# One order for every engine from a plan instead of a table of slots, in a kernel of attention and two feed-forward blocks

## The chip, the cores and the metric

One Trainium2 core runs the whole program; nothing is exchanged with other cores. The time is the device time of one execution in microseconds (us). TensorE does the matrix products, VectorE and ScalarE the elementwise work and the reductions along a row, GpSimd small operations and a reduction over partitions; SyncE and GpSimd issue most of the DMA transfers. Each engine takes its instructions strictly in the order in which the program was written for it, and waits at the first that is not ready.

## The reference

```python
def _attn_ref(q, k, v):                      # 4 batches, 8 heads, 576 rows, 64 columns, f32
    q_rot, k_rot = (rotate(q), rotate(k))    # rotary embedding over the two halves of a row
    scores = scale * np.matmul(q_rot, k_rot.transpose(0, 1, 3, 2))
    scores = scores - np.max(scores, axis=-1, keepdims=True)
    attn = np.exp(scores)
    attn = attn / (np.sum(attn, axis=-1, keepdims=True) + 1e-09)
    return np.matmul(attn, v)

def _moe_ref(x, mu_k, mu_r, w_k, w_v, w_r):  # x is 4 x 576 x 512, w_k 512 x 1024, w_v 1024 x 512
    xk = mu_k * x + (1.0 - mu_k) * x_prev    # x_prev: x moved down by one row
    xr = mu_r * x + (1.0 - mu_r) * x_prev
    k = np.maximum(xk @ w_k, 0.0)
    v = k * k @ w_v
    return 1.0 / (1.0 + np.exp(-(xr @ w_r))) * v

def _moe2_ref(x, w_in, w_spatial, b_spatial, w_out):
    h = np.maximum(x @ w_in, 0.0)
    u, v = (h[..., :512], h[..., 512:])
    v_n = (v - mu) / np.sqrt(var + 1e-06)    # mean and variance of a row
    v_s = np.einsum('ts,bsd->btd', w_spatial, v_n) + b_spatial[None, :, None]
    return u * v_s @ w_out
```

## The kernel before

The program has two phases. The first, which the change is about, does attention and the products with w_k and w_v; the second does the rest and is written out further down in both kernels alike.

**Attention** goes by units. There are 72: 18 for each batch, and one holds 128 rows of a pair of heads (units 8 and 9 of a batch take the last 64 rows of two pairs each). Unit m takes these steps. `scores` (L244, TensorE) writes two PSUM tiles `s`; `top` (L250, VectorE) takes the largest value of each row, once for each head; `expo` (L255, ScalarE) the exponential; `norm` (L260, L261) the reciprocal of the row's sum; `high` (L267, ScalarE) and `low` (L271, VectorE) write the probabilities as two f16 parts into `p`; `turn` (L276) has SyncE issue a DMA transpose of `p` into `pt`; `values` (L296, TensorE, 36 or 72 matmuls, tile `pv`) multiplies by v; and after some units `gather` (L306 to L318) copies the sums to `xt` and stores them to `xd`. The scores of a unit need both `s` tiles of an earlier unit back, so they wait for its `expo`.

**Each pair of heads** is got ready before its units: `load` brings q and k (tiles `raw_0` and `raw_1`, 576 KB each, issued by GpSimd at L166, for the first pair by SyncE), `rope` (L171, L172, VectorE) rotates them into `rot`; at most two `raw` tiles of a kind of buffer are in use, so a load waits for an earlier `rope`. `v_load` (L176, SyncE) brings v into `vr`; `v_max` (L180, VectorE), a sum over partitions on GpSimd (L181), `v_scale` (L185, L186) and `v_split` (L193 on ScalarE, L194 on VectorE) write it as two f16 parts into `vv`, which SyncE copies to the other half of the partitions (L199, L200).

**The first feed-forward block**, `moe1(b, h)`, runs for one part h of a batch's rows (256 or 320) beside the attention of the next batch: `mix` (L340 to L347) writes `x`; `k_dot` (L355) does the product with w_k in eight groups of twelve matmuls (tile `mk`); `k_square` (L364 to L373) squares and splits into `kk`; `v_dot` (L385, tile `mv`) does the product with w_v; `v_out` copies the result to `vs`, and SyncE stores it (L393, `vd`). `vs` and the first tile of `mix` share three buffers. The 16 pieces of w_k and w_v are loaded as 64-bit words and put together at the start (L101 to L118; their last step, a subtraction, is GpSimd's).

**The order** comes from one list, `agenda`. Each step is added with a slot, a number on one scale for the whole phase, where unit m stands at m: its scores at m - .5, its `low` at m + 1.1, its transpose at m + 1.12, its values at m + 3.05. The list is sorted by slot, and every engine gets its steps in that order. The numbers were written by hand and say nothing about how long a step takes. The extra PSUM tiles `ps_x` serve the first units and give way to the pool `ps_m` of the feed-forward block.

Of the kernel before, what the change touches and what calls it, by code (L numbers as in the profile page):

```python
# [27 lines left out]
NX = 20  # L28
# [3 lines left out]
LAG = 3  # L32
# [4 lines left out]
def raw(ap):  # L37
    return ap.bitcast(F32)


@with_exitstack
def body(ctx: ExitStack, tc, qp, kp, vp, cs, mu_k, mu_r, w_k, w_v, w_r, w_in, w_sp, b_sp, w_out, out):
# [12 lines left out]
    st0p = ExitStack()  # L55
# [3 lines left out]
    ps_pv = att.enter_context(tc.tile_pool(name="ps_pv", bufs=1, space=PSUM, side="right"))  # L59

    moe = ph1.enter_context(tc.tile_pool(name="moe", bufs=1))
# [9 lines left out]
    def load_mix():  # L71
        nc.sync.dma_start(mix4[:, :, 0], mu_k.rearrange("(c p) -> p c", p=128))
        nc.sync.dma_start(mix4[:, :, 2], mu_r.rearrange("(c p) -> p c", p=128))
        for k in (0, 2):
            nc.vector.tensor_scalar(mix4[:, :, k + 1], mix4[:, :, k], -1.0, 1.0, op0=ALU.mult, op1=ALU.add)
    epsc = const.tile([128, 2], F32, name="epsc")
# [63 lines left out]


    agenda = []

    def add(slot, fn):
        agenda.append((slot, len(agenda), fn))

    def steps(gen, slots):
        for s in slots:
            add(s, lambda: next(gen, None))
# [5 lines left out]
    def prep(i, s):  # L155
# [22 lines left out]
        def v_max():  # L178
            vm = t["vm"] = at.tile([128, 4], F32, tag="vm", bufs=2, name=f"vm{i}")
            nc.vector.tensor_reduce(vm[:, 0:1], t["vr"], axis=AX.XY, op=ALU.max, apply_absolute_value=True)  # L180
            nc.gpsimd.partition_all_reduce(vm[:, 1:2], vm[:, 0:1], channels=128, reduce_op=bass_isa.ReduceOp.max)  # L181

        def v_scale():
            vm = t["vm"]
            nc.vector.tensor_scalar(vm[:, 2:3], vm[:, 1:2], 1e-30, 1.0 / P_SCALE, op0=ALU.max, op1=ALU.mult)  # L185
            nc.vector.reciprocal(vm[:, 3:4], vm[:, 2:3])  # L186
            nc.gpsimd.tensor_scalar(musc[:, b, p, :], mix4[:, p, :], vm[:, 2:3], 1.0 / P_SCALE, op0=ALU.mult, op1=ALU.mult)

        def v_split():
# [3 lines left out]
            nc.scalar.mul(v5[:, :, 0:D], vr, vm[:, 3:4])  # L193
            nc.vector.scalar_tensor_tensor(v5[:, :, D:], vr, vm[:, 3:4], v5[:, :, 0:D],  # L194
# [12 lines left out]
        todo = []  # L207
        for w in range(2):
            r = at_rope(2 * p + w)
            todo += [(r - 2, load, 1 - w, 0), (r - 1.99, load, 1 - w, 1), (r, rope, 1 - w)]  # L210
        todo += [(s - 3.5, v_load), (s - 2.57, v_max), (s - .57, v_scale), (s - .56, v_split), (s - .55, v_copy)]
        if i == 0:

            todo = [(-9, load, 1, 0), (-8.9, load, 1, 1), (-8.8, load, 0, 0), (-8.7, load, 0, 1), (-8.6, v_load),
                    (-8.5, rope, 1), (-8.4, rope, 0), (-8.3, v_max), (-2.6, load_mix), (.43, v_scale), (.44, v_split),
                    (.45, v_copy)]
        for d, fn, *arg in todo:
            add(d, lambda fn=fn, arg=arg: fn(*arg))
# [14 lines left out]
    def scores(m):  # L233
        ps = [(ps_x if n < NX and n % 3 == 2 else ps_s).tile([128, 2, 512], F32, tag="s", name=f"s{n}")
# [47 lines left out]
    def values(m):  # L282
        b, w = divmod(m, UN)
        pt = units.pop(m)
        if w in (0, 4, 8, 10, 14):
            pvt[0] = (ps_x if m == 4 else ps_pv).tile([128, 512], F32, tag="pv", name=f"pv{m}")
# [12 lines left out]
    def gather(m):  # L299
# [3 lines left out]
        for p in range(NP) if w == 9 else (0, 1) if w in (3, 13) else (2, 3):  # L303
# [5 lines left out]
            if w < 9:  # L309
                for h, (_, n) in enumerate(PART):  # L310
                    xt[i, h] = xpool.tile([128, 1 + n], F32, tag=f"xt{h}", bufs=NP, name=f"xt{i}_{h}")
                nc.gpsimd.memset(xt[i, 0][:, 0:1], 0.0)
                nc.scalar.copy(xt[i, 0][:, 1:], src)
                nc.gpsimd.tensor_copy(xt[i, 1][:, 0:1], xt[i, 0][:, 256:])
                nc.gpsimd.dma_start(x_dram[b][:, p, :257], xt[i, 0])
            else:
                nc.scalar.copy(xt[i, 1][:, 65:], src)
                nc.gpsimd.dma_start(x_dram[b][:, p, 257:], xt[i, 1][:, 1:])  # L318
# [7 lines left out]

    def ps_m():
        if "ps_m" not in pool:
            st0p.close()
            pool["ps_m"] = ph1p.enter_context(tc.tile_pool(name="ps_m", bufs=3, space=PSUM))  # L330
        return pool["ps_m"]
# [17 lines left out]
    def k_dot(b, h, fc):  # L349
        xh, xl = mo[b, h, "x"]  # L350
        ps = mo[b, h, "k", fc] = ps_m().tile([128, 512], F32, tag="m", name=f"mk{b}_{h}_{fc}")
        m = 0
        for c in range(NP):
# [23 lines left out]
    def v_dot(b, h, dc, half):  # L377
        if half == 0:
            mo[b, h, "v", dc] = ps_m().tile([128, 512], F32, tag="m", name=f"mv{b}_{h}_{dc}")
        ps = mo[b, h, "v", dc]  # L380
        m = 12 * half
        for fc in range(4 * half, 4 * half + 4):
# [5 lines left out]
    def v_out(b, h, dc):  # L388
# [4 lines left out]
        nc.sync.dma_start(v_dram[b][:, dc, o:o + n], vs)  # L393

    def moe1(b, h):

        end = UN * b + LAG + (17 if h else 7)
        s, places = end + 1.6, 16 if h else 20
        at_ = lambda m: s + .5 * int(m * places / 16)
        for c in range(NP):  # L400
            m = (end - 3.5 if c < 2 else end) + (c % 2)
            steps(mix(b, h, c), (end + .2, end + .41, end + .95, end + 1.08) if c == 2 else
                  (end + .42, end + .55, end + 1.2, end + 1.41) if c == 3 else (m + .21, m + .41, m + .96, m + 1.09))

        def after(t):

            f = round((t % 1) * 10)
            n = int(t)
            return [n + x for x in ((.95, 1.08, 1.2, 1.4) if f == 1 else (1.2, 1.4, 1.95, 2.08))]

        for fc in range(NFC):
            m = at_(fc)
            add(m, lambda fc=fc: k_dot(b, h, fc))
            steps(k_square(b, h, fc), after(m))
        for k, (dc, half) in enumerate(((0, 0), (1, 0), (0, 1), (1, 1), (2, 0), (2, 1), (3, 0), (3, 1))):
            m = at_(8 + k)
            add(m, lambda dc=dc, half=half: v_dot(b, h, dc, half))
            if half:
                add(after(m)[0], lambda dc=dc: v_out(b, h, dc))


    N = B * UN
    for i in range(B * NP):
        prep(i, UN * (i // NP) + 2 * (i % NP))
    for m in range(N):
        add(m - .5, lambda m=m: scores(m))
        for j in range(2):
            add(m + .01 * j, lambda m=m, j=j: top(m, j))
            add(m + .02 + .01 * j, lambda m=m, j=j: expo(m, j))
            add(m + .35 + .01 * j, lambda m=m, j=j: high(m, j))  # L430
            add(m + 1.1 + .01 * j, lambda m=m, j=j: low(m, j))
        add(m + .3, lambda m=m: norm(m))
        add(m + 1.12, lambda m=m: turn(m))
        add(m + LAG + .05, lambda m=m: values(m))
        if m % UN in (3, 7, 9, 13, 17):
            add(m + LAG + .18, lambda m=m: gather(m))
# [6 lines left out]
    for c in range(16):  # L443
# [6 lines left out]
        for fn, d in zip(fns, (-3.5 if c < 12 else -.6, .21, .45, 1.22, 1.23)):  # L450
            add(c + d, fn)
# [3 lines left out]
    cut = N + LAG + .5  # L455
    agenda.sort(key=lambda t: t[:2])
    with tc.manual_schedule():
        for slot, _, fn in agenda:
            if slot > cut and "p2" not in pool:
                pool["p2"] = 1  # L460
                att.close()
            fn()
# [250 lines left out]
```

## Time and profile before

| | |
|---|---|
| median of three runs | 860.26 us (858.5 to 864.52) |
| the profiled execution | 867.71 us, of which the span is 865.9 us |
| mean granted TensorE clock | 0.932 of full speed |
| first scores of units 0, 12, 30, 48 and 66 | at 10.97, 113.60, 254.42, 378.79 and 506.68 us |

Unit 12 stands just before the first product of the feed-forward block; 30, 48 and 66 stand at the same place one, two and three batches later. The last matmul of the first phase ends at about 588.7 us.

### The profile page before, as it was taken

To read this page: it belongs to the slowest core of one execution; us is meant where nothing else is said; L and a number is where in the kernel's file an instruction comes from. 1 tells how busy PE (TensorE), PEld (TensorE's weight loads), DVE (VectorE), ACT (ScalarE), POOL (GpSimd) and SP (SyncE) were. 2 spreads that over 40 slices of the span, in tenths; PEclk is the share of its full clock that TensorE was granted. 3 is DMA by queue.
4 is the path that set the end of the run, shared out by engine and by line. 5 is a ranking of instruction groups with operands and counts; after the bars stand their busy time and mean duration, and the time that the engine had idled before them with its cause. 6 is when DMAs were issued, how large, how long until landed. Compare 5 with 4: busy or idle time off the path is not lost.

```text
span 865.9 us, 16909 instructions
## 1 busy us (share of the span) xinstructions
PE 742.3 (86%) x6872; PEld 639.6 (74%) x6872; DVE 544.4 (63%) x935; ACT 483.3 (56%) x980; POOL 118.0 (14%) x201
## 2 busy tenths in 40 slices
PE   1445687788999789999688999896989999999998
PEld 0223466576887667787567888896888999998997
DVE  4866988876758777679676656476865334344311
ACT  0645777566757547767457778686743433443211
POOL 1122222211010110011011000124301000101000
PEclk9996878788999789999898999998999999999999
DMA  7766786786589796699875566758430112110101
GB/s 266 207 149 141 143 214 172 167 170 144 108 177 180 164 209 111 124 199 183 175 173 115 102 129 118 204 158 246 138 97 14 59 52 69 52 31 1 42 15 56
DMA packets 197553, 114.20 MB, mean 132 GB/s; under 512 B 172961, under 2 KB 177057, under 8 KB 197474
## 3 DMA queue, kind: packets, MB, share of 16 engines
q1 hardware_dynamic: 191474, 90.10, 47.6%
q0 software_dynamic: 5856, 22.43, 8.5%
q8 instruction: 54, 0.88, 0.4%
q10 hardware_dynamic: 144, 0.59, 0.2%
q14 instruction: 25, 0.20, 0.1%
HBM read 52.26 MB, written 14.16 MB: 77 GB/s over the span
## 4 chain that ended last, share of the span: by engine, by line
PE 45%; DVE 8%; DMA 8%; ACT 7%; issue 2%; SPq 0%; POOL 0%; ACTq 0%; DVEq 0%
PE sp L484 7%; PE o L484 6%; PE mk L355 6%; PE s L244 5%; PE mv L385 5%; PE r L484 5%; PE hv L558 5%; PE u L484 4%; PE pv L296 3%; DMA vr<-vp 2%; DMA vd<-vs 2%; DVE sm L250 1%; ACT p L267 1%; DVE raw L171 1%; ACT pf L255 1%
## 5 line engine op out<-in xcount | busy, mean ns | idle before, releaser
L244 PE MATMUL s<-rot,rot 64*128 64x288 f32 (+1 forms) x640 | 140.4, 493 | 100.4 <-ACT pf L255 88.3
L244 PEld LDWEIGHTS s<-rot,rot 64*128 64x128 f32 (+1 forms) x640 | 73.1, 203 | 141.5 <-ACT pf L255 107.6
L255 ACT ACTIVATE pf<-s,sm 128x576 f32<-128x576 f32 x144 | 105.3, 736 | 129.6 <-DVE sm L250 129.2
L355 PE MATMUL mk<-x,wk 128*128 128x256 f32 (+1 forms) x768 | 126.9, 318 | 1.0 <-ACT x L345 0.6
L385 PE MATMUL mv<-kk,wv 128*128 128x256 f32 (+1 forms) x768 | 122.2, 312 | 3.8 <-POOL wv L118 3.8
L355 PEld LDWEIGHTS mk<-x,wk 128*128 128x128 f32 x768 | 111.9, 201 | 17.4 <-issue 11.9
L385 PEld LDWEIGHTS mv<-kk,wv 128*128 128x128 f32 x768 | 109.0, 198 | 17.3 <-issue 11.0
L250 DVE TENSOR_REDUCE sm<-s 128x1 f32<-128x576 f32 x144 | 102.3, 750 | 29.2 <-PE s L244 29.1
L267 ACT ACTIVATE p<-pf,sm 128x576 f16<-128x576 f32 x144 | 103.9, 772 | 27.4 <-issue 11.2
L271 DVE SCALAR_TENSOR_TENSOR p<-pf,sm,p 128x576 f16<-128x576 f32 x144 | 110.7, 810 | 0.0
L296 PEld LDWEIGHTS <-vv 128*64 128x64 f16 x2880 | 88.2, 122 | 23.9 <-issue 20.3
L296 PE MATMUL pv<-pt,vv 128*64 128x128 f16 (+1 forms) x2880 | 99.5, 231 | 4.7 <-DMA pt<-p 4.7
L484 PE MATMUL r<-xr,wr 128*128 128x288 f32 x384 | 54.8, 302 | 2.5 <-DVE xr L488 1.9
L484 PEld LDWEIGHTS r<-xr,wr 128*128 128x128 f32 x384 | 53.3, 194 | 3.4 <-DVE xr L488 2.2
L558 PE MATMUL hv<-wi,x 128*128 128x512 f32 x192 | 49.5, 407 | 6.9 <-ACT x L487 6.9
L484 PEld LDWEIGHTS u<-x,wi 128*128 128x128 f32 x384 | 53.5, 192 | 1.3 <-ACT us L592 0.3
L484 PE MATMUL u<-x,wi 128*128 128x288 f32 x384 | 54.3, 300 | 0.0
L484 PE MATMUL sp<-ws,vn 128*128 128x288 f32 x384 | 53.9, 295 | 0.0
L484 PE MATMUL o<-g,wo 128*128 128x288 f32 x384 | 52.9, 296 | 0.5 <-ACT os L614 0.5
L484 PEld LDWEIGHTS sp<-ws,vn 128*128 128x128 f32 x384 | 52.4, 188 | 0.7
L484 PEld LDWEIGHTS o<-g,wo 128*128 128x128 f32 x384 | 51.7, 188 | 1.4 <-ACT os L614 1.2
L171 DVE TENSOR_TENSOR raw<-raw,cst 128x1152 f32<-128x1152 f32 x32 | 44.2, 1380 | 13.3 <-DMA raw<-kp 11.6
(295 smaller groups left out, 843.5 us busy)
## 6 DMA issues: line engine op xcount, KB each, us to landing
raw<-kp POOLq DMA_DIRECT2D x15, 576.0 KB, 5.4
raw<-qp POOLq DMA_DIRECT2D x15, 576.0 KB, 6.1
vr<-vp SPq DMA_DIRECT2D x16, 320.0 KB, 5.9
v<-vd SPq DMA_DIRECT2D x16, 288.0 KB, 2.8
out<-os SPq DMA_DIRECT2D x16, 288.0 KB, 2.1
vv<-vv SPq DMA_DIRECT2D x32, 128.0 KB, 2.3
x<-xd SPq DMA_DIRECT2D x12, 288.5 KB, 4.0
xd<-xt POOLq DMA_DIRECT2D x16, 160.0 KB, 6.4
```

Source lines behind the costliest of these rows:

```text
L171: nc.vector.tensor_tensor(x, x, cst, op=ALU.mult)
L244: nc.tensor.matmul(o, q[r, c:c + n], k[r, h * HALF:(h + 1) * HALF], start=True, stop=True)
L250: nc.vector.tensor_reduce(sm[:, 0, j:j + 1], ps[j], axis=AX.XY, op=ALU.max, negate=True)
L255: nc.scalar.activation(pf[j].rearrange("p (a b) -> p a b", a=2), ps[j], AF.Exp, bias=sm[:, 0, j:j + 1], scale=1.0, accum_out=sm[:, 1, j:j ...
L267: nc.scalar.mul(p16[:, j, 0, :], pf[j], sm[:, 3, j:j + 1])
L271: nc.vector.scalar_tensor_tensor(p16[:, j, 1, :], pf[j], sm[:, 3, j:j + 1], p16[:, j, 0, :], op0=ALU.mult, op1=ALU.subtract)
L296: nc.tensor.matmul(pv[HEAD[j], o:o + n], preps[i]["vv"][:, kc, j, D * hl:D * hl + D], a, start=kc + hl == 0, stop=kc + hl == NKC)
L355: nc.tensor.matmul(ps[:, :PART[h][1]], wk[c][fc // 4][:, w, fc % 4 * 128:fc % 4 * 128 + 128], a[:, c, :], start=m == 0, stop=m == 11)
L385: nc.tensor.matmul(ps[:, :PART[h][1]], wv[fc][:, w, dc * 128:(dc + 1) * 128], a, start=m == 0, stop=m == 23)
L484: nc.tensor.matmul(ps[:, h, :HALF], w, a[:, h * HALF:(h + 1) * HALF], start=m == 0, stop=m == n - 1)
L558: nc.tensor.matmul(ps[:, :FS], x[a][:, d, c:c + 128], wi[w][:, d, FS:], start=k == 0, stop=k == 11)
```

## The change

The slots are gone. Every step is now added to a `Plan` with a rank, its engine, a time in us, the steps whose results it needs, the buffers that it takes and uses, and for a DMA the time on the transfer engines. `Plan.order` goes through a made-up clock: whenever an engine is free, it takes the first step in order of rank (among the next 80) whose needs are met and whose buffers are free, and so passes over steps that are not ready. All transfers share one queue there. The steps are then written out in the order in which they started, and this fixed order is what the engines run; at run time nothing is passed over.

Steps were cut finer: `k_dot` and `v_dot` come in chunks of six matmuls (twelve before), `v_max`, `v_scale`, `v_split`, `gather` and `v_out` are taken apart at the engine's border, and the store of `vs` is a step of its own. All loads of q and k are issued by SyncE. `ps_x` is gone, and `ps_m` is there from the start. The number of instructions and of bytes stays as it was.

```diff
+class Plan:
...
+    HOP = .15
...
+    def order(self):
...
+            for engine, xs in todo.items():
+                if free.get(engine, 0.) > now:
+                    continue
+                for k, x in enumerate(xs[:80]):
+                    rank, _, _, us, fn, name, needs, take, use, dma = x
+                    t = max([done.get(n, 1e9) for n in needs], default=0.)
+                    tags = [tag for tag, _ in take]
+                    if t > now:
+                        soon.append(t)
+                    elif all(self.room[tag] >= tags.count(tag) for tag in tags):
+                        for tag in tags:
+                            self.room[tag] -= 1
+                        end = free[engine] = now + us
+                        if dma:
+                            queue = max(queue, end + 1.2) + dma
+                            end = queue + .5
...
-    ps_x = st0p.enter_context(tc.tile_pool(name="ps_x", bufs=1, space=PSUM))
...
-                nc.gpsimd.dma_start(t["raw", which], (qp, kp)[which][b, p])
+                nc.sync.dma_start(t["raw", which], (qp, kp)[which][b, p])
...
-        todo += [(s - 3.5, v_load), (s - 2.57, v_max), (s - .57, v_scale), (s - .56, v_split), (s - .55, v_copy)]
...
+        add(s - 5, "SP", .1, v_load, ("vl", i), needs=pace(s - 5), take=[("vr", ("vr", i))], dma=1.2)
+        add(s - 3.5, "DVE", .8, v_max, ("vmax", i), needs=[("vl", i)], use=[("vr", i)], take=[("vm", ("vm", i))])
+        add(s - 3.4, "POOL", 8., v_all, ("vall", i), needs=[("vmax", i)], use=[("vm", i)])
...
-        m = 0
-        for c in range(NP):
+        m = 6 * half
+        for c in range(2 * half, 2 * half + 2):
...
-        add(m - .5, lambda m=m: scores(m))
...
+        add(m + .7, "SP", .1, lambda m=m: turn(m), ("turn", m),
+            needs=[("low", m, 0), ("low", m, 1)] + [("turn", m - 1)][:m], use=[("p16", m)],
+            take=[("pt", ("pt", m))], dma=3.4)
...
+        add(m + 1.5, "PE", 1.15, lambda m=m: values(m), ("pv", m),
...
-    agenda.sort(key=lambda t: t[:2])
+    order = plan.order()
```

How the order moves is seen in three places. The names end in a number that tells instances apart; it differs between the kernels.

The queue of SyncE before, around the transposes of units 30 to 34, where v of pairs 8 and 9 (`vr`) is loaded:

```order
L276 DMA_TRANSPOSE pt_3075<-p_2987 128x18x128
L276 DMA_TRANSPOSE pt_3156<-p_3083 128x18x128
L176 DMA vr_3168<-vp 128x640
L276 DMA_TRANSPOSE pt_3252<-p_3164 128x18x128
L276 DMA_TRANSPOSE pt_3335<-p_3257 128x18x128
L176 DMA vr_3351<-vp 128x640
L276 DMA_TRANSPOSE pt_3441<-p_3347 128x18x128
```

The same queue after the change, transposes of units 28 to 30, with the same two loads of v and the loads of q and k that GpSimd issued before:

```order
L474 DMA vd_85<-vs_1_3_2874 128x320
L230 DMA vr_2890<-vp 128x640
L220 DMA raw_1_2892<-kp 128x1152
L350 DMA_TRANSPOSE pt_2912<-p_2720 128x18x128
L220 DMA raw_0_3051<-qp 128x1152
L350 DMA_TRANSPOSE pt_3073<-p_2888 128x18x128
L230 DMA vr_3144<-vp 128x640
L220 DMA raw_1_3150<-kp 128x1152
L350 DMA_TRANSPOSE pt_3174<-p_3042 128x18x128
```

The loads of v moved ahead by four units; loads of q and k now stand between the transposes, and those behind them cannot be issued before them.

VectorE before, at the place where v of pair 9 (`vr_3351`) is first read, after the scores of unit 35 (`sm_3359` belongs to unit 35, `p_3347` to unit 34):

```order
L250 TENSOR_REDUCE sm_3359<-s_3354 128x1
L373 TENSOR_TENSOR kk_0_7_3380<-rl_0_6_3288,kk_0_7_3380 128x2x256
L271 SCALAR_TENSOR_TENSOR p_3347<-pf_0_3292,sm_3270,p_3347 128x576
L271 SCALAR_TENSOR_TENSOR p_3347<-pf_1_3294,sm_3270,p_3347 128x576
L260 TENSOR_SCALAR sm_3359<-sm_3359 128x2
L261 RECIPROCAL sm_3359<-sm_3359 128x2
L185 TENSOR_SCALAR vm_3261<-vm_3261 128x1
L186 RECIPROCAL vm_3261<-vm_3261 128x1
L180 TENSOR_REDUCE vm_3451<-vr_3351 128x1
```

VectorE after the change, around unit 31 (`sm_3039`; `p_3042` belongs to unit 30):

```order
L324 TENSOR_REDUCE sm_3039<-s_3033 128x1
L345 SCALAR_TENSOR_TENSOR p_3042<-pf_0_3009,sm_2873,p_3042 128x576
L345 SCALAR_TENSOR_TENSOR p_3042<-pf_1_3019,sm_2873,p_3042 128x576
L324 TENSOR_REDUCE sm_3039<-s_3034 128x1
L450 TENSOR_TENSOR kk_0_3_3075<-rl_0_2_3029,kk_0_3_3075 128x2x256
L225 TENSOR_TENSOR raw_1_2892<-raw_1_2892,cst 128x1152
L226 TENSOR_TENSOR rot_1_3126<-raw_1_2892 128x576
```

`low` of unit 30 is done before the rotation of `raw_1_2892`, while the load into the buffer that this rotation frees (`raw_1_3150`) stands ahead of unit 30's transpose in SyncE's queue. Pair 9's v (`vr_3144`) is first read only after the scores of unit 33.

GpSimd before, at the start: the sum over partitions for pair 2 (`vm_241`, an ISA instruction of its own around it), the weights' last step (`wk`) and loads:

```order
L187 TENSOR_SCALAR musc<-mix_91,vm_157 128x4
L181 ISA
L181 ISA vm_241<-vm_241 128x1
L118 ISA
L118 TENSOR_TENSOR wk_100<-I-222_223,wk_100 128x512
L166 DMA raw_0_285<-qp 128x1152
L118 TENSOR_TENSOR wk_102<-I-271_272,wk_102 128x512
```

And after the change, the sums for pairs 2 and 3 (`vm_267`, `vm_371`):

```order
L174 TENSOR_TENSOR wk_100<-I-212_213,wk_100 128x512
L174 TENSOR_TENSOR wk_102<-I-221_222,wk_102 128x512
L238 ISA
L238 ISA vm_267<-vm_267 128x1
L247 ISA
L247 TENSOR_SCALAR musc<-mix_91,vm_267 128x4
L174 TENSOR_TENSOR wk_104<-I-263_264,wk_104 128x512
L238 ISA
L238 ISA vm_371<-vm_371 128x1
L174 ISA
L174 TENSOR_TENSOR wk_99<-I-273_274,wk_99 128x512
```

Two more pieces of weights now come before the sum for pair 2, and only one stands between it and the sum for pair 3.

## Rows read from the trace of the kernel before

**Rows 1.** Windows, six stages: us, busy us by engine, granted clock, DMA share.

```profile
0.00:116.50 116.50, 54.19 (x480) 34.58 (x480) 82.27 (x137) 61.19 (x124) 24.72 (x42) 0.87 0.71 181
116.50:255.60 139.10, 120.75 (x1266) 98.63 (x1265) 103.39 (x173) 90.45 (x194) 24.20 (x39) 0.86 0.74 162
255.60:380.00 124.40, 112.64 (x1267) 91.49 (x1265) 91.76 (x164) 81.59 (x180) 13.87 (x32) 0.93 0.81 163
380.00:507.85 127.85, 114.19 (x1266) 92.22 (x1264) 92.16 (x164) 82.33 (x181) 13.05 (x30) 0.93 0.77 153
507.85:588.70 80.85, 77.11 (x834) 71.59 (x833) 51.13 (x81) 62.55 (x131) 13.11 (x12) 1.00 0.64 158
588.70:865.90 277.20, 263.43 (x1770) 251.10 (x1768) 123.64 (x217) 105.16 (x172) 29.03 (x47) 0.97 0.20 65
```

**Rows 2.** Timeline of TensorE: start, us, line, tiles, idle before.

```profile
10.97 3.24 PE L244 MATMUL s<-rot,rot 64*128 64x288 f32 x10 [10.97 <-DVE rot L172]
...
62.16 2.29 PE L244 MATMUL s<-rot,rot 64*128 64x288 f32 x6 [10.64 <-ACT pf L255]
...
81.30 2.28 PE L244 MATMUL s<-rot,rot 64*128 64x288 f32 x6 [7.98 <-ACT pf L255]
...
113.60 3.01 PE L244 MATMUL s<-rot,rot 64*128 64x288 f32 x8 [2.04 <-ACT pf L255]
...
254.42 1.24 PE L244 MATMUL s<-rot,rot 64*128 64x288 f32 x8
...
378.79 1.24 PE L244 MATMUL s<-rot,rot 64*128 64x288 f32 x8
...
506.68 1.24 PE L244 MATMUL s<-rot,rot 64*128 64x288 f32 x8
```

**Rows 3.** Timelines of GpSimd and, last, ScalarE, in the start.

```profile
53.20 1.25 POOL L118 TENSOR_TENSOR wk<-I-222_223,wk 128x512 fp32r<-128x512 f32 x1 [7.42 <-issue]
...
177.12 0.52 POOL L181 PARTITION_ALL_REDUCE vm<-vm  x1 [6.29 <-issue]
...
54.49 0.66 ACT L106 ACTIVATE I-348_349<-I-167_168 128x512 f32<-128x512 f32 x1 [7.91 <-POOL wk L118]
```

**Rows 4.** Chain of waits, 270 to 345 us: start, us, what.

```profile
275.26 4.18 DMA vr<-vp
...
287.78 5.81 DMA vr<-vp
...
309.22 1.62 PE mv L385 x12
...
317.74 7.45 DMA vd<-vs
...
339.64 1.17 PE s L244 x8
340.81 1.96 PE mk L355 x12
342.76 1.13 PE pv L296 x36
```

**Rows 5.** Groups of instructions, VectorE: count, busy us, mean ns, idle before.

```profile
L271 DVE SCALAR_TENSOR_TENSOR p<-pf,sm,p 128x576 f16<-128x576 f32 x144 | 110.7, 810 | 0.0
...
L250 DVE TENSOR_REDUCE sm<-s 128x1 f32<-128x576 f32 x144 | 102.3, 750 | 29.2 <-PE s L244 29.1
...
L171 DVE TENSOR_TENSOR raw<-raw,cst 128x1152 f32<-128x1152 f32 x32 | 44.2, 1380 | 13.3 <-DMA raw<-kp 11.6 <-DMA raw<-qp 1.7
...
L172 DVE TENSOR_TENSOR rot<-raw 128x576 f32<-128x576 f32 x32 | 24.3, 759 | 1.1
```

**Rows 6.** Timeline of SyncE's queue, 262 to 335 us.

```profile
277.74 9.98 SPq L276 DMA_TRANSPOSE pt<-p  x2
...
301.01 2.49 SPq L276 DMA_TRANSPOSE pt<-p  x1
```

**Rows 7.** DMA queue of GpSimd, 255.6 to 380 us: packets, MB, engines' share.

```profile
q0 software_dynamic: 1537, 5.92, 15.8%
```

More of the change, by code (lines that the diff above doesn't have):

```diff
@@ L38, in raw, with __init__, add @@
     return ap.bitcast(F32)
+class Plan:
+    HOP = .15
+    def __init__(self, room):
+        self.room, self.steps, self.users, self.tag = dict(room), [], {}, {}
+    def add(self, rank, engine, us, fn, name, needs=(), take=(), use=(), dma=0):
+        self.steps.append((rank, len(self.steps), engine, us, fn, name, tuple(needs), tuple(take), tuple(use), dma))
+        for tag, buf in take:
+            self.tag[buf] = tag
+        for buf in [x for _, x in take] + list(use):
+            self.users[buf] = self.users.get(buf, 0) + 1
+    def order(self):
+        todo, free, done, left, queue, now, out = {}, {}, {}, dict(self.users), 0., 0., []
+        for x in sorted(self.steps):
+            todo.setdefault(x[2], []).append(x)
+        back = []
+        while any(todo.values()):
+            for end, bufs in [x for x in back if x[0] <= now]:
+                back.remove((end, bufs))
+                for buf in bufs:
+                    left[buf] -= 1
+                    if not left[buf]:
+                        self.room[self.tag[buf]] += 1
+            soon = []
+            for engine, xs in todo.items():
[14 more added lines that the diff above has]
+                            end = queue + .5
+                        done[name] = end + self.HOP
+                        back.append((end + self.HOP, [b for _, b in take] + list(use)))
+                        out.append((now, x))
+                        del xs[k]
+                        break
+            later = [t for t in [*soon, *free.values(), *(x[0] for x in back)] if t > now]
+            assert min(later, default=1e9) < 1e9, "no step can start: " + str([xs[:2] for xs in todo.values()])
+            now = min(later)
+        self.ends = done
+        return out
@@ L138, in body, with pace @@
     HEAD = slice(0, 64), slice(64, 128)
[L142 to L149, printed above, removed]
+    plan = Plan(dict(raw=RAW, rot=ROT, vr=2, vm=2, vv=VVS, s=2, sm=4, pf=PFS, p16=P16S, pt=PTS, pvb=1, xt0=NP, xt1=NP,
+                     x=1, mf=3, rl=2, kk=4, wg=2, m=3))
+    add = plan.add
+    def pace(rank):
+        return [("s", int(rank) - 1)] if rank >= 1 else [("rope", 0, 0)] if rank > -2.7 else []
     UN = 9 * NP // 2
@@ L233, in scores @@
     def scores(m):
[L234 removed]
+        ps = [ps_s.tile([128, 2, 512], F32, tag="s", name=f"s{n}")
               for n in (2 * m, 2 * m + 1)]
@@ L400, in moe1 @@
         for c in range(NP):
[L401 to L409, printed above, removed]
+            i = b * NP + c
@@ L423, in body @@
+    add(-2, "DVE", .4, mix_less, "mix", needs=["mu"])
     for i in range(B * NP):
@@ L425, in body @@
     for m in range(N):
-        add(m - .5, lambda m=m: scores(m))
-        for j in range(2):
[L428 to L436, printed above, removed]
+        b, w = divmod(m, UN)
```

178 lines of the change are left out of this document (135 added, 43 removed).

## The prediction

> **What bounds the kernel now.** I read the windows by stage first [rows 1]. The second phase (277.20 us of the span, TensorE busy for 263.43) is TensorE's, and the change does not touch it. The 588.7 us ahead of it are the case. In the two middle batches the windows show four resources at nearly the same load: of 124.40 us, TensorE is busy for 112.64 at a clock of 0.93, VectorE for 91.76, ScalarE for 81.59, and the transfer engines at a share of 0.81, so 101 us. No engine is full, and none is far from it: what is lost is lost in waits. In the first stage (116.50 us) VectorE is busy for 82.27 and TensorE hardly.
>
> The timeline of TensorE gives the pace [rows 2]: first scores of unit 0 at 10.97, of units 12, 30, 48 and 66 at 113.60, 254.42, 378.79 and 506.68. So the start takes 113.6, the first eighteen units beside a feed-forward block 140.8, the next two rounds 124.4 and 127.9, and from unit 66 to the end of the phase 82.0.
>
> The chain of waits says what the loss is made of [rows 4]: in one round it passes through two loads of v (4.18 and 5.81) and a store of `vs` (7.45). That is 17.4 us in which a slot stood too close behind the transfer it needs; the next round has the same three steps. In the start ScalarE waits 7.91 for a buffer that GpSimd's subtraction must free, and that subtraction sits behind a sum over partitions, after which GpSimd stands for 7.42 without a releaser [rows 3]; TensorE's idle times of 10.64 and 7.98 are this stall and its repetition two units later [rows 2].
>
> **What the order alone is worth.** I walked through both orders unit by unit, gave each instruction its duration from the groups and the chain (twelve matmuls 1.62 or 1.96, scores 1.17, values 1.13 [rows 4]; on VectorE `low` 0.81, `top` 0.75, a rotation 1.38 and 0.76 [rows 5], taken 0.08 shorter where one follows on the other), and summed per engine. For units 30 to 47 that gives TensorE 99.8, VectorE 91.4 and ScalarE 83.9 in both kernels, close to the windows' 91.76 and 81.59, so the sums can be trusted. Then I took blocks of two units, and in each the engine with the most work. These sums of the largest are bounds that hold if nothing waits:
>
> - units 0 to 11: 82.0 before, 85.7 after (one rotation and one piece of weights more stand ahead of unit 12);
> - units 12 to 29: 115.0 before, 112.7 after;
> - units 30 to 47: 110.6 before, 109.8 after; units 48 to 65: 110.6 and 110.1;
> - unit 66 to the end, TensorE alone: 58.1 before, 54.0 after, since more of the block is done by then.
>
> So the finer chunks and the new mixing are worth next to nothing by themselves: the order stays dense in some units and without feed-forward work in three or four others. The change pays only by the waits. Before, the stages lie above their bounds by 20.6 (113.6 - 10.97 - 82.0), 25.8, 13.8 and 17.3 us.
>
> **The waits that go.** Loads of v stand three or four units further ahead on SyncE and are read one to three units earlier, so that most have gained one unit or two, 7 to 14 us by the rounds; the longest in the chain took 5.81. The store of `vs` is passed over until its copy is there, and the tiles that share its buffers come later. That covers the 17.4 us, all of the 13.8 and 17.3. In the start three subtractions now stand ahead of the sum for pair 2, and ScalarE's next steps are laid out around it.
>
> **The waits that come.** First, the queue of SyncE. Of the 30 whole loads of q and k that move there, 18 hold nothing up. Twelve stand ahead of a transpose that is ready earlier, since the rotation that frees their buffer stands behind `low` on VectorE. The delay is what VectorE has between the two: from 2.1 us (one rotation) over 3.6 (a `top`, a split, a rotation) to 8.5 for unit 16; by the durations above 46 us for the twelve. Each load then also has its own data in front of the transpose. GpSimd's queue took 15.8% of 124.40 us for 5.92 MB [rows 7], eight loads of q and k being 4.72 MB of it: 2.0 us each, 24 for the twelve. Behind the transpose wait `values` and everything after it on TensorE; but in both orders the values of a unit stand behind the scores of the third unit after it, some 20 us by the rounds, so I count a third of the 70 us, 24: 7 a round, 10 in units 12 to 29, where six of the twelve stand at its beginning.
>
> That the transfer engines share their time is visible: beside GpSimd's loads two transposes keep SyncE for 9.98, a single one in a quiet stretch for 2.49 [rows 6]. [...]
>
> Second, GpSimd in the start. The plan gives the sum over partitions 8.0 us. The rows show 7.42 after it and, where GpSimd comes from other work, 6.29 ahead of it [rows 3], so 14 where the two do not fall into an idle time. Between the sums for pairs 2 and 3 only one subtraction stands, and the weights after them wait for both. I leave 8 us of the start's 20.6 for that, about one such stall. Third, the first rotation now waits for the second halves of q and k, with two loads of v ahead of them: one more us, by VectorE's first operations and the loads' size, between 0 and 3.
>
> **The sum**, stage by stage, against the profiled execution: start 12.0 + 85.7 + 8 = 105.7 for 113.6, gain 7.9; units 12 to 29, 112.7 + 10 = 122.7 for 140.8, gain 18.1; units 30 to 47, 109.8 + 7 = 116.8 for 124.4, gain 7.6; units 48 to 65, 110.1 + 7 = 117.1 for 127.9, gain 10.8; the end 3 of the 4.1, as the second phase's weights must still come in beside it. Together 47 us: 867.7 becomes 820.7. The profiled execution lies 7.5 us above the median of the runs, 860.3, so I take 813.
>
> **The rivals.** *The transposes' delays reach TensorE, and its clock falls each time* (slower): nothing absorbs the 70 us, of which 24 are counted: 813 + 46 = 859. After such a stop TensorE runs at the lower of its two levels: unit 12's scores took 3.01, unit 30's 1.24 [rows 2], and twelve matmuls behind them would lose as much again, some 3.4 us for each of twelve stops, 41 in all: 900. For it speaks that SyncE runs strictly in order and that the transfer share is 0.81 already; against it the three units between a unit's scores and its values. It is slower than before by more than 1% once 80 of the 111 us arrive.
>
> *The waits only move* (no change): the bounds are alike, so if the fixed order finds other late steps as often as the table did, what is left is the bounds' own difference, 3 us: 857. For it speaks that the plan's times are guesses that run-time order cannot mend, against it that the three waits in the chain have each a plain cause which is gone.
>
> *Nothing waits* (more gain): all the 8 + 10 + 7 + 7 go too: 781. Against it: the transfer engines' 101 us of 124.4 leave little room for a round under 110.
>
> **How the numbers follow.** The forecast has a chance of 0.65, and a range of its own from 797 to 845 (its kept waits halved, or doubled); the waits that move 0.12, nothing waits 0.10, the delays in full 0.13. Runs of this kernel differ by 0.7%, so 1% is about what a measurement can tell from no change. Faster by over 1% is the forecast and the third rival, 0.75; within 1% 0.12; slower 0.13. The range 782 to 868 leaves out the slower rival and half of the best one.
>
> **What would show it.** In the profile after, unit 12's scores near 106, and rounds of about 117; no load of v and no store of `vs` of several us in the chain; TensorE's granted clock in the middle rounds at or above 0.93. If values wait for `pt` by more than some 7 us a round, the first rival is at work; if `musc` or `wk` on GpSimd hold ScalarE in units 4 to 7 for more than 8 us together, the start was mis-sized. The second phase should stay at 277 us; if it does not, the sum is wrong in a place that I held fixed.

## The result and the profile after

The changed kernel takes 818.32 us (median of four runs, 817.79 to 820.15), the kernel before in the same runs 861.65: a ratio of 0.950, 95% interval 0.946 to 0.954. The forecast was 813. The profiled execution took 818.47, of which the span is 816.7. The two profiled executions are thus 49.2 us of span apart and the medians 43.3, since that of the kernel before (867.71) lies 6.1 above its median; what is said by stage below is the difference of the profiled two.

The windows of the profile after, cut where the first scores of units 12, 30, 48 and 66 begin and where the first phase ends (the columns are those of [rows 1]):

```profile
0.00:105.40 105.40, 54.82 (x498) 35.11 (x498) 88.23 (x141) 65.16 (x129) 26.77 (x36) 0.82 0.88 222
105.40:229.20 123.80, 109.23 (x1254) 89.60 (x1252) 100.63 (x171) 85.70 (x187) 16.16 (x28) 0.91 0.80 166
229.20:345.15 115.95, 106.56 (x1266) 88.23 (x1265) 91.82 (x166) 83.63 (x180) 11.03 (x24) 0.94 0.81 175
345.15:458.85 113.70, 108.12 (x1283) 90.00 (x1282) 90.68 (x164) 83.15 (x183) 10.50 (x24) 0.95 0.88 169
458.85:541.00 82.15, 76.18 (x817) 70.47 (x817) 53.92 (x82) 64.18 (x131) 13.96 (x12) 0.98 0.67 160
541.00:816.70 275.70, 261.62 (x1765) 249.32 (x1763) 123.11 (x217) 105.16 (x173) 29.36 (x47) 0.98 0.20 64
```

Against the unit starts of [rows 2] the gains are 8.2 us in the start (7.9 forecast), 17.0 in units 12 to 29 (18.1), 8.4 and 14.2 in the two rounds (7.6 and 10.8), nothing in the end (3) and 1.5 in the second phase (0). In the rounds VectorE and ScalarE work as long as before, within 2.1 us; TensorE is busy for 106.56 us where it was 112.64 in the first of them.

The chain of waits between 294 and 326 us, which answers to [rows 4]:

```profile
294.65 1.00 PE mk L432 x5
295.65 1.17 PE s L318 x8
296.83 1.07 PE mk L432 x6
297.90 1.13 PE pv L370 x36
299.03 1.96 PE mk L432 x12
...
319.95 2.83 PE mv L462 x18
322.78 1.13 PE pv L370 x36
323.91 1.96 PE mv L462 x12
```

From 294.65 to unit 48 it is TensorE without a break, and no load of v and no store of `vs` stands in it. The chain of this profile begins only at 289 us, in the middle of the round; for both whole rounds the waits speak. All waits of the kernel before for these transfers (what ended the waits, us, times, longest):

```profile
DVE vm L180 <- DMA vr<-vp: 15.5, 7, 4.6
ACT vs L392 <- DMA vd<-vs: 13.5, 4, 3.7
```

and after:

```profile
DVE vm L234 <- DMA vr<-vp: 6.5, 2, 6.3
ACT vs L469 <- DMA vd<-vs: 0.7, 1, 0.7
```

Of the 6.5 us none lies in the two rounds. In the second round the chain leaves TensorE twice, for 16 us mostly of VectorE's work from 380.8 on and for a transpose of 6.30. The page's costliest groups show what TensorE still waits for (busy us, mean ns, then idle before and its releaser):

```profile
L318 PE MATMUL s<-rot,rot 64*128 64x288 f32 (+1 forms) x640 | 129.1, 481 | 55.6 <-ACT pf L329 41.9
...
L370 PE MATMUL pv<-pt,vv 128*64 128x128 f16 (+1 forms) x2880 | 100.1, 232 | 17.0 <-DMA pt<-p 16.9
```

Before, the scores' idle time was 100.4 us, of which 88.3 for the exponentials, and values waited 4.7 for `pt`. The waits for `pt` are 6.8, 4.4 and 4.2 us in the stages from unit 12 to 65, below the 7 a round that the forecast named as a sign of the first rival. So far all is as forecast. The experiments say that it is so for other reasons.

### The profile page after: what moved, and what is told of

It reads as the page before. It is cut to its first block, busy times and chain, and to the rows that moved or that the text cites. A ratio compares the mean times of both kernels' runs of the same rounds, so it can differ in the third digit from the quotient of the medians.

```text
span 816.7 us, 16914 instructions
## 1 busy us (share of the span) xinstructions
PE 716.5 (88%) x6872; PEld 622.7 (76%) x6872; DVE 548.4 (67%) x935; ACT 487.0 (60%) x980; POOL 107.8 (13%) x171
## 4 chain that ended last, share of the span: by engine, by line
PE 50%; DVE 4%; ACT 4%; DMA 4%; issue 1%; POOL 0%; DVEq 0%; ACTq 0%; SPq 0%
PE sp L625 7%; PE mv L462 6%; PE mk L432 6%; PE o L625 6%; PE s L318 5%; PE hv L699 5%; PE r L625 5%; PE u L625 5%; PE pv L370 4%; DMA pt<-p 1%; DMA I-8206_8207<-w_sp 1%; DMA I-8247_8248<-w_out 1%; DMA I-7579_7580<-w_in 1%; DMA I-7623_7624<-w_in 1%; DVE sm L324 1%
## 5 line engine op out<-in xcount | busy, mean ns | idle before, releaser
L318 PE MATMUL s<-rot,rot 64*128 64x288 f32 (+1 forms) x640 | 129.1, 481 | 55.6 <-ACT pf L329 41.9
L329 ACT ACTIVATE pf<-s,sm 128x576 f32<-128x576 f32 x144 | 106.2, 739 | 58.7 <-DVE sm L324 57.9
L318 PEld LDWEIGHTS s<-rot,rot 64*128 64x128 f32 (+1 forms) x640 | 66.9, 199 | 91.9 <-ACT pf L329 55.9
L432 PE MATMUL mk<-x,wk 128*128 128x256 f32 (+1 forms) x768 | 121.0, 307 | 12.0 <-ACT x L420 7.1
L341 ACT ACTIVATE p<-pf,sm 128x576 f16<-128x576 f32 x144 | 109.4, 771 | 36.6 <-DVE sm L335 17.5
L324 DVE TENSOR_REDUCE sm<-s 128x1 f32<-128x576 f32 x144 | 107.0, 751 | 34.9 <-PE s L318 34.6
L345 DVE SCALAR_TENSOR_TENSOR p<-pf,sm,p 128x576 f16<-128x576 f32 x144 | 118.9, 833 | 17.2 <-ACT p L341 17.1
L432 PEld LDWEIGHTS mk<-x,wk 128*128 128x128 f32 x768 | 107.3, 193 | 25.0 <-ACT x L420 7.9
L462 PE MATMUL mv<-kk,wv 128*128 128x256 f32 (+1 forms) x768 | 117.9, 302 | 1.5 <-DVE kk L450 1.5
L462 PEld LDWEIGHTS mv<-kk,wv 128*128 128x128 f32 x768 | 104.8, 189 | 14.1 <-issue 10.3
L370 PE MATMUL pv<-pt,vv 128*64 128x128 f16 (+1 forms) x2880 | 100.1, 232 | 17.0 <-DMA pt<-p 16.9
L699 PEld LDWEIGHTS hv<-wi,x 128*128 128x128 f32 x192 | 35.9, 192 | 14.7 <-ACT x L628 6.9
```

The costliest lines, as they stand in the source:

```text
L318: nc.tensor.matmul(o, q[r, c:c + n], k[r, h * HALF:(h + 1) * HALF], start=True, stop=True)
L324: nc.vector.tensor_reduce(sm[:, 0, j:j + 1], ps[j], axis=AX.XY, op=ALU.max, negate=True)
L329: nc.scalar.activation(pf[j].rearrange("p (a b) -> p a b", a=2), ps[j], AF.Exp, bias=sm[:, 0, j:j + 1], scale=1.0, accum_out=sm[:, 1, j:j ...
L341: nc.scalar.mul(p16[:, j, 0, :], pf[j], sm[:, 3, j:j + 1])
L345: nc.vector.scalar_tensor_tensor(p16[:, j, 1, :], pf[j], sm[:, 3, j:j + 1], p16[:, j, 0, :], op0=ALU.mult, op1=ALU.subtract)
L370: nc.tensor.matmul(pv[HEAD[j], o:o + n], preps[i]["vv"][:, kc, j, D * hl:D * hl + D], a, start=kc + hl == 0, stop=kc + hl == NKC)
```

## The experiments

### One part undone: where the loads are issued

```diff
-                nc.sync.dma_start(t["raw", which], (qp, kp)[which][b, p])
+                nc.gpsimd.dma_start(t["raw", which], (qp, kp)[which][b, p])
```

> The changed kernel, the 30 whole loads of q and k issued by GpSimd as before the change, at the same place in the plan. Theory A (loads that stand ahead of a transpose on SyncE hold it, and that costs the 7 us a round that the forecast kept): the waits of values for pt fall from 16.9 us to under 8, and 806 to 814 us. Rival C (the move to SyncE is a gain, since q and k land after 4.7 us in place of 5.4 to 6.1 and GpSimd is free): 825 to 835 us, with VectorE waiting for raw. Between, 815 to 822: the move is worth nothing either way.

Measured: 838.19 us (ratio to before 0.970, 0.967 to 0.974), 20 above the changed kernel. The start takes 117.0 us in place of 105.4, the two rounds 119.4 and 117.2. So the loads gain on SyncE, where I had them cost: my theory has the sign wrong. Values wait for `pt` for 23.0 us, but 5.5 of these lie in the start; from unit 12 on it is 17.5 where the changed kernel has 16.9, and in both the waits of over 1 us there come before the values of the same units, 17, 18, 34, 35, 50, 52 and 70. They do not hang on who issues the loads. The holds on SyncE that I had counted did come in the changed kernel (line, what ended the waits, us, times, longest):

```profile
SPq L220 <- DVE rot L226: 21.1, 8, 5.2
```

They do not show in what TensorE waits for. Rival C holds by its second reason, that GpSimd is free: VectorE waits for `raw` only 4.6 us in all. GpSimd's timeline in the start shows how:

```profile
21.07 0.55 POOL L220 DMA_DIRECT2D raw<-kp  x1 [6.33 <-DVE rot L226]
31.12 0.26 POOL L247 TENSOR_SCALAR musc<-mix,vm 128x4 f32<-128x4 f32 x1 [9.50 <-issue]
31.46 1.26 POOL L174 TENSOR_TENSOR wk<-I-190_191,wk 128x512 fp32r<-128x512 f32 x1
...
39.88 0.60 POOL L220 DMA_DIRECT2D raw<-kp  x1
48.82 0.38 POOL L238 PARTITION_ALL_REDUCE vm<-vm  x1 [8.34 <-issue]
49.08 0.74 POOL L220 DMA_DIRECT2D raw<-qp  x1
59.28 0.40 POOL L247 TENSOR_SCALAR musc<-mix,vm 128x4 f32<-128x4 f32 x1 [9.46 <-DVE sm L324]
59.76 1.69 POOL L174 TENSOR_TENSOR wk<-I-263_264,wk 128x512 fp32r<-128x512 f32 x1
```

The same engine in the changed kernel:

```profile
21.27 0.26 POOL L247 TENSOR_SCALAR musc<-mix,vm 128x4 f32<-128x4 f32 x1 [9.80 <-DVE rot L226]
24.19 1.66 POOL L174 TENSOR_TENSOR wk<-I-190_191,wk 128x512 fp32r<-128x512 f32 x1 [2.66 <-ACT wk L171]
...
40.04 0.38 POOL L238 PARTITION_ALL_REDUCE vm<-vm  x1 [6.16 <-DVE p L345]
47.37 0.26 POOL L247 TENSOR_SCALAR musc<-mix,vm 128x4 f32<-128x4 f32 x1 [6.95 <-DVE p L345]
47.71 1.26 POOL L174 TENSOR_TENSOR wk<-I-263_264,wk 128x512 fp32r<-128x512 f32 x1
```

A load of k waits 6.33 us for its buffer. Only behind it begin the 9.50 us in which GpSimd stands without a releaser; in the changed kernel the like stall of 9.80 begins right behind the sum. So `musc` comes 9.9 us later, and with two more loads on the way the weights' fourth subtraction (`I-263_264`) comes 12.1 us later. ScalarE, whose buffers these free, waits three times:

```profile
32.76 0.66 ACT L162 ACTIVATE I-221_222<-I-156_157 128x512 f32<-128x512 f32 x1 [7.34 <-POOL wk L174]
...
61.48 0.66 ACT L162 ACTIVATE I-386_387<-I-251_252 128x512 f32<-128x512 f32 x1 [7.32 <-POOL wk L174]
76.19 0.66 ACT L162 ACTIVATE I-505_506<-I-342_343 128x512 f32<-128x512 f32 x1 [8.08 <-POOL wk L174]
```

In the changed kernel the same three are 0.65 us, nothing and 3.74.

The loads of batch 0 by SyncE, those of the other batches by GpSimd:

```diff
-                nc.sync.dma_start(t["raw", which], (qp, kp)[which][b, p])
+                (nc.gpsimd if b else nc.sync).dma_start(t["raw", which], (qp, kp)[which][b, p])
```

> The changed kernel with the loads of q and k of batches 1 to 3 by GpSimd and those of batch 0 by SyncE. If the 20 us that GpSimd's loads cost (838 against 818) come from the start, where GpSimd also sums over partitions and ScalarE waits for wk (7.3, 7.3 and 8.1 us): unit 12 near 105 and 823 to 829 us, the rest, some 3.5 a round, staying. If they come from the transfers themselves (q and k landing later, beside the transposes, in every round): 832 to 840. Theory A as forecast (loads ahead of transposes cost) had it below 818.

Measured: 827.62 us; unit 12 at 105.0. So batch 0's loads account for 10.6 of the 20 us, and the start falls by 12.0. The other 9.3 lie in the two rounds (120.2 and 118.6); which wait makes them is not settled, since the control below moves the rounds nearly as far. Values wait 11.4 us for `pt` here, less than with all loads on SyncE, and at no other units.

The table before, its loads on SyncE:

```diff
-                nc.gpsimd.dma_start(t["raw", which], (qp, kp)[which][b, p])
+                nc.sync.dma_start(t["raw", which], (qp, kp)[which][b, p])
```

> The kernel before, with its table, and only the loads of q and k moved to SyncE, at their slots. If the move pays by itself, because GpSimd's queue in the start holds loads and weights up: 845 to 855 us, unit 12 near 103. If on a table the loads hold transposes behind them, as the forecast had it, and only a plan can place them: 860 to 885, with values waiting for pt well over the 4.7 us of before.

Measured: 849.91 us (0.984, 0.980 to 0.989), 13 below before, with 108.0 us for the start and 131.9 for units 12 to 29 (113.6 and 140.8 before); the rounds, 125.9 and 126.2, gain nothing together. Values wait 3.6 us for `pt`, not more than before. The move pays without any plan, and holds no transpose that TensorE waits for.

### One part undone: the halves

The two halves of a chunk become one step again (here the first product; the second likewise, and what names the steps):

```diff
-            for k in range(2):
-                add(m + .1 * k, "PE", .9 * f, lambda fc=fc, k=k: k_dot(b, h, fc, k), ("k", P, fc, k),
...
+            add(m, "PE", 1.8 * f, lambda fc=fc: k_dot(b, h, fc), ("k", P, fc),
...
```

> The changed kernel with whole chunks: a chunk of the first product is one step of twelve matmuls again, and so are the halves of the second, planned at 1.8 times f us; all else as after the change. Theory A (the bounds of both orders differ by next to nothing, so finer chunks are worth little): 816 to 824 us. Rival B (halves fill gaps that whole chunks cannot): 830 to 850 us, with TensorE's wait of scores for the exponentials well above 42 us.

Measured: 830.02 us (0.962, 0.958 to 0.966), 11.7 above the changed kernel, so the halves are worth more than I gave them. The same with GpSimd's loads as well, which leaves the plan alone (with the pools and the finer steps around the chunks that belong to it):

> The plan alone: the changed kernel with whole chunks and with the loads of q and k by GpSimd, so that only the order (and the pools and distances that belong to it) differs from before. By the two runs apart (loads 20 us, halves 12), if their effects add: 850 us, so the order alone is worth 14 of the 46. If they overlap: 838 to 845, and the order alone is worth more than half. Theory A, all from the order: 818 to 825, already spoken against by the two runs.

Measured: 852.82 us (0.988, 0.984 to 0.992). Step by step: plan alone 10, halves 14.6 on top (838.19), loads 19.9 (818.32). In the other order, loads on the table 13, plan 19.9 (830.02), halves 11.7. Halves and loads nearly add, while the plan is worth 10 with GpSimd's loads and twice that with SyncE's. The sets of runs differ a little (the kernel before has medians from 861.65 to 864.25 in them); by the ratios to it the halves are worth 9.8 to 15.1 us and the loads under the plan 17.3. TensorE's scores and values in the round of units 30 to 47 (busy us, mean ns, idle before) show what the halves do; whole chunks, all else changed:

```profile
L318 PE MATMUL s<-rot,rot 64*128 64x288 f32 (+1 forms) x162 | 33.6, 488 | 7.6 <-ACT pf L329 7.4
L370 PE MATMUL pv<-pt,vv 128*64 128x128 f16 (+1 forms) x720 | 24.6, 230 | 1.9 <-ACT mf L415 1.9
```

and the changed kernel:

```profile
L318 PE MATMUL s<-rot,rot 64*128 64x288 f32 (+1 forms) x161 | 27.6, 446 | 2.8 <-ACT pf L329 2.8
L370 PE MATMUL pv<-pt,vv 128*64 128x128 f16 (+1 forms) x720 | 24.3, 228 | 4.4 <-DMA pt<-p 4.4
```

With whole chunks TensorE stands 7.6 us in front of scores, and the scores take 33.6 us against 27.6. The window of that round with whole chunks, and the stretch of it in which the clock was at 0.50, the lower of its two levels (the other is 1.00; columns as in [rows 1]):

```profile
227.90:349.40 121.50, 112.04 (x1267) 91.03 (x1268) 92.39 (x165) 83.54 (x181) 9.06 (x24) 0.89 0.80 167
272.80:300.10 27.30, 20.95 (x146) 13.62 (x147) 22.51 (x42) 17.07 (x35) 3.08 (x7) 0.50 0.76 152
```

In the changed kernel's round there are two such stretches:

```profile
276.60:280.10 3.50, 3.04 (x40) 2.87 (x41) 3.47 (x5) 1.37 (x4) 0.49 (x1) 0.51 0.94 201
283.50:293.70 10.20, 7.42 (x74) 5.02 (x68) 7.47 (x15) 6.40 (x15) 1.82 (x4) 0.50 0.63 131
```

The granted clock of the round is 0.89 for 0.94; in the pair of runs with GpSimd's loads it is 0.89 and 0.94 as well, and the scores fall from 32.6 to 27.5 us. Over all executions of the two pairs the mean clock is 0.912 to 0.926 with whole chunks and 0.928 to 0.945 with halves. TensorE's busy time falls by 5.5 us (112.04 to 106.56), as much as the 5.4 that the round gains; its idle time stays at 9.5 and 9.4. So what the halves save in this round is not idle time but time at the lower level. My bounds had priced every matmul alike in both orders.

What TensorE did before the clock fell stands in its timeline, first with whole chunks and then in the changed kernel:

```profile
264.89 1.69 PE L462 MATMUL mv<-kk,wv 128*128 128x256 f32 x12
...
274.23 1.32 PE L318 MATMUL s<-rot,rot 64*128 64x288 f32 x2 [3.81 <-ACT pf L329]
...
298.38 4.55 PE L432 MATMUL mk<-x,wk 128*128 128x320 f32 x24
```

```profile
269.77 2.76 PE L432 MATMUL mk<-x,wk 128*128 128x320 f32 x17 [1.42 <-DVE x L422]
...
293.29 0.59 PE L432 MATMUL mk<-x,wk 128*128 128x320 f32 x1
```

Between the two parts of a feed-forward block the plan leaves TensorE with scores and values alone, which stop for the exponentials and for `pt`: for 31.8 us with whole chunks, for 20.8 with halves (34.9 and 22.9 in the other pair). A first half needs two of the four pieces of `x`, a whole chunk all four, so with halves the next part's first product begins before this gap. Whether that earlier start or the smaller piece as such makes the gain was not tried apart.

The halves cut again, into steps of three matmuls (`.45 * f` us each):

> The changed kernel with its chunks in quarters (steps of three matmuls) where it has halves. If halves gain because a smaller piece lets the next scores start sooner and leaves fewer stops without feed-forward work (scores' waits for the exponentials 7.6 us in the round of units 30 to 47 with whole chunks, 2.8 with halves), quarters gain again, but less than the 12 us of the halves: 808 to 815. If the halves had their gain from the one order that the plan happened to find: 818 to 832.

Measured: 814.39 us (0.941, 0.939 to 0.944), the rounds 113.7 and 112.2, both at a clock of 0.97. That lies in the range of the first answer; how far it is one order's luck is said at the control below.

### Passing over taken away

```diff
-                for k, x in enumerate(xs[:80]):
+                for k, x in enumerate(xs[:1]):
```

> The changed kernel, its plan looking at one step per engine only: each engine takes its steps in the order of their ranks and passes over nothing; halves, loads by SyncE and buffers stay. Theory A (the gain is the waits that passing over removes): the ranks are then a table again, and waits for late steps come back in every stage, 840 to 880 us, with TensorE's wait of scores for the exponentials (41.9 us after the change, 88.3 before it) back at 70 or more. Rival B (the halves of the chunks and the new ranks bring the gain, passing over next to nothing): 815 to 830 us, and that wait stays near 42.

Measured: 1073.44 us. The ranks put values only one and a half units behind their scores' unit, so with nothing else in front each waits for its transpose (line, what ended the waits, us, times, longest):

```profile
PE pv L370 <- DMA pt<-p: 268.4, 71, 9.9
```

That is a bad table more than a test of passing over. Still in strict order, but with the distance of the table before:

```diff
-        add(m + 1.5, "PE", 1.15, lambda m=m: values(m), ("pv", m),
+        add(m + 3.05, "PE", 1.15, lambda m=m: values(m), ("pv", m),
```

> The changed kernel in strict rank order again, but with a distance that a table would keep: values 3.05 units behind their scores' unit, gathers, stores and mixing as far behind. TensorE's order in the middle rounds is then that of the table before, with SyncE's loads, and the other engines go by the new ranks. Theory A (passing over brings the gain): 840 to 865 us, near the kernel before. Rival (the loads on SyncE and the new ranks bring it, and only the distance of values failed in the strict order that took 1073 us): 815 to 832.

Gathers, stores and mixing are set as far behind. Measured: 860.76 us, within half a per cent of the kernel before (0.996, 0.994 to 0.999), rounds 124.9 and 125.5. Halves, new ranks and new pools in a strict order are worth nothing, and the 13 us of the loads are lost again. Theory A holds in this: the other parts pay only where the order may give way, or, for the loads, on the old table. Passing over with values at 3.05 was not run, so passing over and the closer ranks that it allows are not told apart.

### The chain's waits, taken out of the table

```diff
-        todo += [(s - 3.5, v_load), (s - 2.57, v_max), ...
+        todo += [(s - 4.5, v_load), (s - 2.57, v_max), ...
-        vs = moe_tile([128, PART[1][1]], F32, "mf", 3, name=...)[:, :n]
+        vs = moe_tile([128, PART[1][1] if dc > 1 else 512], F32, *(("mf", 3) if dc > 1 else ("wg", 2)), name=...)[:, :n]
```

> The kernel before, with its table, and two edits that take away the waits of its chain: loads of v stand one slot earlier, and the first two vs of a block have buffers of their own (those of the weights' stages, idle by then), so that no copy waits for a store. Theory A (these waits, 17.4 us in a round of 124.4, are what the rounds lost): 825 to 838 us, the two middle rounds near 113 to 118. Rival (the waits only move: the next late step takes their place): 850 to 860 us, rounds still above 121, and the chain shows other waits of the same size.

Measured: 853.62 us (0.987, 0.983 to 0.991), 10.3 below before; rounds 121.1 and 118.8. Before, the chain of the second round held three transfers: loads of v with 3.88 and 7.48 us, a store of `vs` with 7.40. Now (371 to 490 us) one is left, a load of q:

```profile
428.74 5.76 issue
...
435.03 4.97 DMA raw<-qp
```

Ahead of it GpSimd stands for 5.76 us at a sum over partitions before it issues that load. So 18.8 us of transfers left the chain of that round and 10.7 of another kind came in, and 9.1 left its time; in the first round, with the 17.4 of [rows 4], 3.2. These are differences of profiled executions, which lie 18.8 us of span apart where the medians differ by 10.3, so they are rather too large. Scores wait 78.1 us for the exponentials in place of 88.3. The rival holds for more than half: the next late step was close behind.

### The plan's prices, and a control

The transpose at 3.0 us of SyncE in place of 0.1:

> The changed kernel; the plan gives a transpose 3.0 us of SyncE in place of 0.1, so that a load no longer seems free beside it (the rows have SyncE held 2.4 to 5.8 us by one). Theory A, what is left of it (TensorE's 16.9 us of waits for pt come from loads ahead of transposes in an order that the plan thought free): those waits fall under 10 and 808 to 816 us. Rival (a transpose's wait for pt is the transfers' own speed, whatever stands ahead): 815 to 824, the waits for pt still 14 to 22.

Measured: 904.98 us (1.048, 1.044 to 1.052), rounds 139.9 and 135.1, and 17.8 us of waiting for `pt`, as much as without the edit. Neither theory had the time. The edit counts the transpose twice, since the plan gives it 3.4 us of transfer behind the 3.0. The order then sets other work ahead: in 60 of 72 units the values stand behind the scores of the fifth unit after (of the third in 54 after the change), and VectorE waits 69.9 us for scores in place of 34.6. Which of this costs the time was not tried.

The sum over partitions at 14 us in place of 8:

> The changed kernel; the plan gives the sum over partitions 14 us of GpSimd in place of 8, what the rows show with the stalls on both sides of it. Theory A (8 us of the start are kept by that): unit 12's scores come at 98 to 103 in place of 105.4, and 811 to 816 us. Rival (the start is bounded by VectorE's and ScalarE's work there, and the stall falls beside it): unit 12 between 104 and 108, 816 to 822.

Measured: 814.64 us (0.943, 0.940 to 0.946). Unit 12 comes at 104.4, as the rival has it, but unit 30 at 221.3 in place of 229.2 (228.6 in the control): some 8 us, but a stage later than theory A has them. The rounds, 117.5 and 117.4, give most of it back, as the control's do. Neither theory is settled by it.

The plan's `HOP` at .2 in place of .15:

> A control: the changed kernel with the plan's time between engines at 0.2 us in place of 0.15, a change without a meaning, which still gives another order on every engine. It shows what an order of the same kind costs by chance: within 3 us of the 818, and differences of 10 us between plans are effects; 8 us or more away, and a single plan variant shows little.

Measured: 822.04 us (818.07 to 825.43; 0.951, 0.946 to 0.955), rounds 119.6 and 117.2 for 115.95 and 113.70. That is 3.7 us by the medians, but nothing by the ratios (0.951 and 0.950), since the kernel before is also slower in this set of runs; and the rounds are those of the longest of four executions. So differences of 10 us and more stand. Quarters and the longer sum, each 4 below the changed kernel, are 7.7 and 7.4 below this control in the same set of runs, with intervals of the ratio that do not meet: they are faster than this one throw of the plan. But the longer sum gained where no theory had it, so an order can find as much by chance, and one throw does not tell the quarters from that.

## Why the prediction was right, and where it was not

**The time, the sign and the stages** came as forecast, the stages within 3.4 us each, 813 for 818.32. The closeness by stage is in part luck: the control moves a round by 3.7, and the stages here are those of a profiled execution before that was itself 6.1 us over its median.

**The bounds** stood: 115.95 and 113.70 lie 6.2 and 3.6 us above 109.8 and 110.1, where 7 were kept.

**"The change pays only by the waits", and "finer chunks are worth next to nothing by themselves": wrong.** The halves are worth 11.7 to 14.6 us of the 45. The step that fails is the sum for TensorE: 99.8 us for units 30 to 47 in both kernels, where the window had it busy for 112.64; only VectorE's and ScalarE's sums were held against the windows. A good part of what it leaves out is TensorE's time at the lower level of its clock, and that differs between the orders: some 17 us in the round before (by its clock of 0.93), 27.3 with whole chunks under the plan, 13.7 with halves. "By themselves" is right in one sense: in strict rank order they brought nothing.

**The waits that go.** That they left the chain is right; that this "covers the 17.4 us" is not. Without them the table's time fell by 10.3 us; in its profile the two rounds are 12.3 shorter, where I had laid all of their 31.1 us above the bounds to such waits and kept 14.

**The queue of SyncE: wrong sign.** I kept 24 us as a cost of the loads there; the move gains 13 on the table and 20 under the plan. The step that fails is the third of the delays that was to reach TensorE: loads did stand on SyncE for rotations (21.1 us), but values wait at the same units, and from unit 12 on as long (16.9 and 17.5 us), when GpSimd issues the loads. The waits for `pt` did grow by the change, from 4.7; with whole chunks they are 7.6, and what makes them was not tried further. The 2.0 us of its own data that each load was to put in front of a transpose are an estimate from [rows 7], and no run shows that term apart: transposes land 6.1 us after their issue (median of 72) where it was 5.2 before, and the move gains all the same. Nor do the 9.98 us of [rows 6] measure what the transfers share: for 5.1 of them SyncE waits for `low`, while GpSimd's queue has 31.2% of the transfer engines' time in that stretch and SyncE's 58.7%. The total came out because the errors cancel: forecast were 47 us from the order alone, 24 for the loads already taken off; measured were, added in this sequence, 10.1 from the order, 14.6 from the halves and 19.9 from the loads.

**The start.** 8.2 for 7.9. The first scores come at 13.37 us, 2.4 later than before, where one us was kept. The wait that was to show it mis-sized did not come: ScalarE waits 3.74 us for `wk` at the last of these places, 7.91 in [rows 3]. What the start gained is GpSimd's queue without loads: 117.0 with them under the same plan, 108.0 without them on the table. Other plans with SyncE's loads have the start between 98.5 and 105.0 us, so that 105.4 is near 105.7 is luck in part. Whether the 8 us kept lie in the sum over partitions stays open.

**The end: the term that was mis-sized.** 3 us forecast, none measured: with the last block's work moved ahead, TensorE waits in the remainder, once 3.5 us for ScalarE's `x`. The second phase gained 1.5 where I held it fixed; that is no more than it varies between runs that leave it alone (271 to 278 us).

**The rivals.** *The delays reach TensorE, and its clock falls*: refuted for the loads, with waits for `pt` of 4.4 and 4.2 us and 0.94 and 0.95 of the clock in the rounds. That a stop lowers the clock each time, no run shows: unit 12's scores of 3.01 us ran at a granted clock of 0.50, but it had stood there since 100 us, ahead of their stop of 2.04 us, and behind the stop of 10.64 us it was 1.00 (62.0 to 64.5 us). *The waits only move*: half true for the waits in the chain, as the repaired table shows. *Nothing waits*: the rounds came within 4 to 6 us of their bounds.

## What to carry to other kernels

Bounds by summed work say what an order can reach, not what a finer step is worth: where TensorE stops often, price its time at the lower level of its clock too, here 27.3 us of a round with whole chunks and 13.7 with halves. A transfer's issue belongs on the queue whose other work can best wait for it; look first at what stands behind it, not at what stands ahead. And before one planner's result is taken for an effect, throw the plan once more with a number that means nothing: here that moved the median by 4 us, and a further edit gained as much where no theory had it. One throw is few, and such small differences are best taken within one set of runs.

## What was not expected of the hardware

GpSimd's stall around a sum over partitions falls on both sides each time the kind of work changes: 6.16 us ahead of it and 6.95 behind in the changed kernel, 5.77 and 6.87 at the next one, 8.34 and 9.46 where GpSimd issues the loads and one stands in between. Around the changed kernel's 16 sums no such change comes without GpSimd standing for at least 5.77 us, while the first two sums, one right behind the other, take 1.40 us together. What makes the stall, no run shows.
